# Gate steps ahead of their group, and decay sums ahead of the feed, in a gated linear attention followed by a maxout network

## The chip, the cores and the metric

The kernel runs on one core of one Trainium2 chip. The metric is the device time of one execution in microseconds (us). The kernel before the change took 739.53 us, the median of three runs (738.25 to 742.4). A core has a matrix engine (TensorE, PE in the profile, with its weight loads as PEld), a vector engine (VectorE, DVE), an engine for activation functions (ScalarE, ACT), a general one (GpSimd, POOL) and a queue that only issues transfers here (SyncE, SP). Each engine works through its own instructions in order; they wait for each other by semaphores.

## The reference

For each of 4 batches and 8 heads, a state of 48 x 48 complex numbers is decayed at every one of 768 time steps by a complex gate and takes up the outer product of a key and a value; the query reads its real part. The result, 3072 tokens of 384 numbers, goes through a maxout network.

```python
mag = np.sqrt(a_re * a_re + a_im * a_im)
scale = np.minimum(mag, 0.999) / (mag + 1e-06)
a_re_n, a_im_n = (a_re * scale, a_im * scale)
for t in range(S):
    ar, ai = (a_re_n[:, :, t, :, None], a_im_n[:, :, t, :, None])
    new_re = ar * S_re - ai * S_im
    new_im = ar * S_im + ai * S_re
    kv = np.einsum('bhd,bhe->bhde', k[:, :, t], v[:, :, t])
    S_re, S_im = (new_re + kv, new_im)
    y[:, :, t] = np.einsum('bhd,bhde->bhe', q[:, :, t], S_re)
# ... x: y as (B*S, H*D)
h = np.maximum(np.maximum(x @ w1, x @ w2), x @ w3)
return h @ w_out
```

## The kernel before

The kernel does not step through time. It works on tiles of 128 time steps, with all heads at once, 24 tiles in all; two tiles make a group, three groups a batch. For each tile the gate becomes a logarithm of its size (Ln, the decay) and an angle counted in turns (w). Sums of both over the time steps, made by matmuls with triangular matrices, turn into factors for k and q: the exponentials En and E of the decay sums, and cosine and sine (CS) of the summed turns. With these, a tile's outputs are matrix products within the tile (scores A and B) and with the state g. The network of the tokens before is fed in between as fillers for TensorE.

The gates come in three steps over both tiles of a group. L, w and e are scratch tiles of which there is only one buffer each; Ln has two.

```python
def gate_steps(g, cs):
    # ...
    def s0():
        # ... takes the buffers L, w, e, Ln
        nc.scalar.activation(out=w, in_=ar, func=AF.Square)
        nc.scalar.activation(out=L, in_=ai, func=AF.Square)
        nc.vector.tensor_tensor(out=L, in0=L, in1=w, op=OP.add)
        nc.vector.tensor_scalar(out=L, in0=L, scalar1=SMALL, scalar2=LARGE, op0=OP.max, op1=OP.min)
        act(out=L, in_=L, func=AF.Ln)

    def s1():
        # ...
        act(out=w, in_=L, func=AF.Exp, scale=0.5)
        act(out=e, in_=L, func=AF.Exp, scale=-0.5)
        act(out=e, in_=e, func=AF.Ln, scale=1e-6, bias=1.0)
        nc.scalar.activation(out=L, in_=L, func=AF.Relu, scale=-0.5, bias=lnmax)
        nc.vector.scalar_tensor_tensor(out=part("Ln"), in0=L, scalar=-LNMAX, in1=e, op0=OP.add, op1=OP.add)

    def s2():
        # ...
        nc.scalar.activation(out=e, in_=ar, func=AF.Abs)
        nc.vector.tensor_tensor(out=w, in0=w, in1=e, op=OP.add)
        act(out=L, in_=w, func=AF.Ln)
        act(out=L, in_=L, func=AF.Exp, scale=-1.0)
        (nc.gpsimd if g > 1 else nc.vector).tensor_tensor(out=ai, in0=ai, in1=L, op=OP.mult)
        nc.vector.tensor_tensor(out=w, in0=w, in1=L, op=OP.mult)
        nc.vector.scalar_tensor_tensor(out=w, in0=w, scalar=2.0, in1=ai, op0=OP.subtract, op1=OP.mult)
        nc.scalar.activation(out=ar, in_=ar, func=AF.Sign, bias=tiny)
        nc.scalar.activation(out=ai, in_=ar, func=AF.Copy, scale=-0.25, bias=0.25)
        nc.scalar.activation(out=ar, in_=ar, func=AF.Copy, scale=-1.0 / math.pi)
        # ... less the carry of the group before
    return [s0, s1, s2]
```

The turns and their sums (the tile cs), between two loads of ScalarE's function tables:

```python
def turns(g, cs, meanwhile):
    # ...
    act(out=w[:, lo:hi], in_=w[:, lo:hi], func=AF.Arctan)
    nc.vector.tensor_tensor(out=w[:, lo:hi], in0=w[:, lo:hi], in1=ar[:, lo:hi], op=OP.mult)
    nc.vector.tensor_tensor(out=w[:, lo:hi], in0=w[:, lo:hi], in1=ai[:, lo:hi], op=OP.add)
    meanwhile(2)              # two up steps of the network
    for c in cs:
        ps = banks("cs", DM)
        # ... matmuls of w with triangles of ones; their fractional parts nf

def angles(g, cs, meanwhile=lambda n: None):
    table("trig_and_small")
    turns(g, cs, meanwhile)
    sines(g, cs)
    table("natural_log_exp_and_others")
```

The decay sums of a tile (s0 of products), their exponentials, and the products with k and q on GpSimd; E has two buffers:

```python
    # ... ps = banks("sums"): matmuls of Ln with mid and rest
    act(out=En..., in_=ps[:, :, HC:2 * HC], func=AF.Exp, scale=-1.0)
    for nm, sg in (("k", 1.0), ("q", -1.0)):
        E = nat2.tile([P, DM], FP, tag="E", name="E")
        act(out=E..., in_=ps[:, :, 0:HC], func=AF.Exp, scale=sg)
        eng = nc.gpsimd if g > 1 else nc.vector
        eng.tensor_tensor(out=hd(T[nm, x]), in0=E, in1=hd(T[nm, x]), op=OP.mult)
```

All these matmuls write to psum tiles from one pool of four. `turned(x)` transposes k and q of a tile (turn), copies them from psum on ScalarE, makes the decay factors f (cut, psum tile F) and the new state (psum tile dk, and uk, which is k with its factor En):

```python
def turned(x):
    if x < NX:
        turn(x, "k")
        turn(x, "q")
        cut(x)
    state(x - 1)
    if x < NX:
        products(x)[2]()
        prep(x, 0)

def feed(n):                 # n steps of the network: an up step (tile up, into hT) or an output step (op)
    for _ in range(min(n, len(ffn))):
        ffn.pop(0)()
```

A group, as the source gives its order. `pre` holds the steps for the group after it. TensorE keeps to the order of the source from the second group of this loop on; on the other engines a scheduler picks among what it takes to be ready, by the order of the source.

```python
def group(g):
    x, y = g * C, g * C + 1
    # ... loads; the list of network steps
    pre = pre_steps(g + 1, feed) if g + 1 < NG else [lambda: None] * 8
    gates, sums, (turning,), units = pre[:3], pre[3:5], pre[5:6], pre[6:]
    # ...
    if g > 1:
        feed(1)
    pairs(x)                 # scores A, B and their gathering
    gates[0]()
    gates[1]()
    feed(1)
    turned(y)
    gates[2]()
    feed(1)
    sums[0]()
    sums[1]()
    outputs(x, tokens(x))    # psum tile y, copied to xT
    rest(y)
    turning()                # angles, with two up steps
    pairs(y)
    units[0]()
    units[1]()
    feed(2)
    turned(y + 1)
    feed(1)
    outputs(y, tokens(y))
    rest(y + 1)
    feed(len(ffn))
```

Of the kernel before, what the change touches and what calls it, by code (L numbers as in the profile page):

```python
# [48 lines left out]
def kernel(  # L49
# [22 lines left out]
    C = 2  # L72
# [4 lines left out]
    NG = B * GB  # L77
# [30 lines left out]
    def act(**kw):  # L108
        tab(nc.scalar.activation(**kw))  # L109
# [14 lines left out]
    def banks(nm, n=None):  # L124

        ps = psum.tile([P, 2, 512], FP, tag="ps", name=nm)
        return ps if n is None else ps.rearrange("p a n -> p (a n)")[:, 0:n]
# [139 lines left out]
    def load(g, *parts):  # L267
        for part in parts if g < NG else ():
            for c in range(C):
                part(g, c)  # L270
# [52 lines left out]
    def flat(t):  # L323
        return t.rearrange("p c h d -> p (c h d)")
# [6 lines left out]
    def gate_steps(g, cs):  # L331
        lo, hi = cs[0] * DM, (cs[-1] + 1) * DM

        def part(nm):
            t = T[nm, g]
            return (flat(t) if len(t.shape) == 4 else t)[:, lo:hi]

        def s0():
            if lo == 0:
                for nm in "Lwe":  # L340
                    T[nm, g] = nat1.tile([P, W], FP, tag=nm, name=nm)
                T["Ln", g] = nat2.tile([P, W], FP, tag="Ln", name="Ln")
            L, w, ar, ai = part("L"), part("w"), part("ar"), part("ai")
# [8 lines that stand above are left out]
            L, w, e = part("L"), part("w"), part("e")  # L352
# [8 lines that stand above are left out]
            L, w, e, ar, ai = part("L"), part("w"), part("e"), part("ar"), part("ai")  # L361
# [12 lines that stand above are left out]
            if lo == 0 and g % GB > 0:  # L374
                nc.gpsimd.tensor_tensor(out=ai[0:1, 0:DM], in0=ai[0:1, 0:DM], in1=T["carry", g], op=OP.subtract)

        return [s0, s1, s2]
# [91 lines left out]
    def turn(x, nm):  # L469
        ps = banks("tp", H * P).rearrange("p (s t) -> p s t", t=P)  # L470
        for n in range(H):
            mt(out=ps[0:DD, n], in_=both(T["U" + nm, x], n), identity=ident)
        src = ps[0:DD]
        if nm == "k":
            T["K", x] = un2.tile([P, H, P], FP, tag="K", name="K")
            nc.scalar.copy(out=T["K", x][0:DD], in_=src)  # L476
        else:

            T["Q", x] = un2.tile([P, 4 * H, 48], FP, tag="Q", name="Q")
            nc.scalar.copy(out=T["Q", x][0:DD, :, 0:32], in_=src.rearrange("p s (a t) -> p (s a) t", a=4))  # L480
# [128 lines left out]
    def outputs(x, xs):  # L609

        atm, V, G, QG = T["atm", x], T["v", x], T["G", x], T["QG", x]
        y = banks("y", DM).rearrange("p (k t) -> p k t", k=KD)
        queues = [[] for _ in range(4)]
        for r in range(DM // 32):
            i, w = divmod(r, 3)
            runs = ((0,), (1, 2), (3,))[w]
            for c in range(2):
                todo = [(n, new) for new in (True, False) for n in runs]
                queues[r % 4] += [(r, c, i, n, new, (n, new) == todo[0], (n, new) == todo[-1]) for n, new in todo]
        for todo in zip(*queues):  # L620
            for r, c, i, n, new, start, stop in todo:
                (j, h), lo = divmod(2 * i + n // 2, 4), 32 * n
                mm(out=y[32 * (r % 4):32 * (r % 4) + 32, r // 4, c * L64:(c + 1) * L64],
                                 lhsT=V[:, c, i, lo:lo + 32] if new else G[0:DD, c, i, lo:lo + 32],
                                 rhs=atm[:, 4 * c + h] if new else QG[0:DD, 2 * (4 * c + h) + j], start=start, stop=stop)
        if x == xs[0]:

            T["xT", xs[-1]] = fp2.tile([P, KD, P], FP, tag="ot", name="xT") if len(xs) == 1 else \
                fp2.tile([P, KD, TG], FP, tag="xT", name="xT")
        o = (x - xs[0]) * P  # L630
        nc.scalar.copy(out=T["xT", xs[-1]][:, :, o:o + P], in_=y)
# [32 lines left out]
    def pre_steps(g, *meanwhile):  # L664
        if g >= NG:
            return []
        cs = list(range(C))
        parts = [products(g * C + c) for c in cs]
        return gate_steps(g, cs) + [p[0] for p in parts] + [call(angles, g, cs, *meanwhile)] + [p[1] for p in parts]

    def tokens(x):

        return [x] if x < C else [x // C * C + c for c in range(C)]

    def ffn_steps(xs):

        n = 2 if xs[0] == 0 else 3
        return [call(up_step, xs, range(f, f + n), i) for f in range(0, KF, n) for i in range(3)] \
            + [call(out_step, xs, x) for x in xs]
# [64 lines left out]
    def group(g):  # L744
        x, y = g * C, g * C + 1
        load(g + 1, load_v)
        load(g + 2, load_a, load_kq)
        ffn = held + ffn_steps(tokens(x - 1))
        held[:] = [ffn.pop()]

        def feed(n):
            for _ in range(min(n, len(ffn))):
                ffn.pop(0)()

        pre = pre_steps(g + 1, feed) if g + 1 < NG else [lambda: None] * 8
        gates, sums, (turning,), units = pre[:3], pre[3:5], pre[5:6], pre[6:]

        def pairs(x):
            for f in (scores, gather):
                for nm in "AB":  # L760
                    f(x, nm)
# [12 lines that stand above are left out]
        def rest(x):  # L774
            if x < NX:
                for p in range(1, 4):
                    prep(x, p)

        if g > 1:
            feed(1)  # L780
        pairs(x)
        gates[0]()
        gates[1]()
        feed(1)
        turned(y)
        gates[2]()
        feed(1)
        sums[0]()
        sums[1]()
        outputs(x, tokens(x))  # L790
        rest(y)
        turning()
        pairs(y)
        units[0]()
        units[1]()
        feed(2)
        turned(y + 1)
        feed(1)
# [4 lines that stand above are left out]
    for g in range(1, NG):  # L803
        if g == 2:
            T["chain"] = None
        group(g)
# [32 lines left out]
```

## Time and profile before

| | before |
|---|---|
| median of three runs | 739.53 us |
| span of the profiled execution | 738.4 us |
| network's up matmuls, TensorE busy | 294.0 us |
| network's output matmuls, TensorE busy | 100.5 us |
| TensorE's waits for the turns w ahead of cs | 53.9 us in 12 waits |
| TensorE's waits for Ln ahead of the decay sums | 21.9 us in 4 waits |

The page divides the span in 40 slices; each digit is the busy share of a slice in tenths, and PEclk the clock that TensorE was granted, in tenths of full speed:

```profile
PE   1255588499899899899899899899999899999998
PEld 0144476378778778778778778678778778778785
DVE  5899898776775785775766776776766776756111
ACT  6678665565665565555655555555555555422000
POOL 9200300501302302301303203102204104100000
PEclk9968799899999999999999999999999999999999
```

The first eight slices or so, some 150 us, are the start: weights are loaded and the first group is prepared. Then come the groups, and in the last slices only the network's matmuls are left. In other views, a row that shows a wait has its length and what ended it in brackets.

### The profile page before, as it was taken

Reading aid. Unit: us, or ns where it says so; the run is one execution under the profiler, and the core shown is the slowest. Engines: PE = TensorE matmul, PEld = TensorE weight load, DVE = VectorE, ACT = ScalarE, POOL = GpSimd, SP = SyncE. Lnnn points to the kernel's source line nnn. Section 1 sums busy time; section 2 is a strip of 40 time slices with the busy share of each in tenths; the row PEclk is TensorE's granted clock in tenths of the full one; section 3 lists DMA queues with packets and bytes.
Section 4 is the critical chain, followed back from the end, with each engine's and each line's share of the span. In section 5 each row is a group of like instructions: output and inputs, shape, how many; then the busy total and the mean of one; then the engine's idle time right before and its main releaser. Section 6 shows DMA issues by size and latency. Waiting matters only on the chain.

```text
span 738.4 us, 25162 instructions
## 1 busy us (share of the span) xinstructions
PE 636.7 (86%) x11196; PEld 521.5 (71%) x11196; DVE 506.1 (69%) x695; ACT 391.5 (53%) x617; POOL 134.8 (18%) x121
## 2 busy tenths in 40 slices
PE   1255588499899899899899899899999899999998
PEld 0144476378778778778778778678778778778785
DVE  5899898776775785775766776776766776756111
ACT  6678665565665565555655555555555555422000
POOL 9200300501302302301303203102204104100000
PEclk9968799899999999999999999999999999999999
DMA  8555452131231230230320230221321030000000
GB/s 207 148 122 147 95 132 44 22 71 33 55 60 24 51 60 23 52 60 22 58 59 23 49 64 21 54 57 24 61 55 24 11 67 3 1 25 3 4 21 21
DMA packets 138285, 39.41 MB, mean 53 GB/s; under 512 B 130880, under 2 KB 133952, under 8 KB 138176
## 3 DMA queue, kind: packets, MB, share of 16 engines
q1 hardware_dynamic: 137664, 37.78, 23.3%
q8 instruction: 88, 1.44, 0.8%
q14 instruction: 21, 0.17, 0.1%
q10 hardware_dynamic: 512, 0.01, 0.0%
HBM read 33.03 MB, written 4.72 MB: 51 GB/s over the span
## 4 chain that ended last, share of the span: by engine, by line
PE 42%; issue 28%; ACT 9%; DVE 8%; POOL 6%; SPq 3%; DMA 3%; POOLq 0%; ACTq 0%; DVEq 0%
PE up L114 18%; PE op L114 8%; PE cs L114 4%; PE y L114 3%; PE tp L114 3%; POOL q L454 2%; PE B L114 2%; DMA vb<-in_v_dram 2%; POOL ai L367 2%; SPq L255 1%; PE dk L114 1%; PE A L114 1%; ACT f L109 1%; ACT L130 1%; POOL k L454 1%
## 5 line engine op out<-in xcount | busy, mean ns | idle before, releaser
L114 PE MATMUL up<-xT,w 128*128 128x256 f32 (+1 forms) x1404 | 294.0, 367 | 5.5 <-DVE hT L649 4.8
L114 PEld LDWEIGHTS up<-xT,w 128*128 128x128 f32 x1404 | 247.3, 190 | 39.8 <-DVE hT L649 5.5
L367 POOL TENSOR_TENSOR ai<-ai,L 128x768 f32<-128x768 f32 x10 | 29.8, 2980 | 420.1 <-ACT L L109 369.3
L114 PE MATMUL op<-wo,hT 128*128 128x384 f32 x288 | 100.5, 499 | 1.5 <-DVE wo L321 1.0
L114 PE MATMUL cs<-w,upto 128*64 128x192 f32 x192 | 35.6, 425 | 53.9 <-DVE w L385 53.9
L649 DVE TENSOR_TENSOR hT<-hT,up 128x768 f32<-128x768 f32 (+2 forms) x54 | 46.5, 861 | 47.1 <-PE up L114 47.0
L114 PEld LDWEIGHTS op<-wo,hT 128*128 128x128 f32 x288 | 53.3, 192 | 35.5 <-DVE wo L321 1.1
L507 DVE TENSOR_TENSOR Q<-Q,f 112x512 f32<-112x512 f32 x48 | 33.0, 689 | 49.9 <-ACT f L109 49.8
L114 PEld LDWEIGHTS cs<-w,upto 128*64 128x64 f32 x192 | 21.9, 174 | 62.6 <-issue 35.8
L647 ACT COPY hT<-up 128x768 f32<-128x768 f32 (+2 forms) x27 | 19.6, 727 | 81.3 <-PE up L114 81.1
L507 DVE TENSOR_TENSOR QB<-Q,f 112x512 f32<-112x512 f32 (+1 forms) x48 | 58.2, 1248 | 0.0
L476 ACT COPY K<-tp 112x1024 f32<-112x1024 f32 x24 | 24.3, 1012 | 45.6 <-PE tp L114 44.9
L114 PE MATMUL y<-QG,g 112*32 112x64 f32 x1536 | 46.9, 222 | 1.0 <-DVE g L607 1.0
L114 PE MATMUL y<-atm,vb 128*32 128x64 f32 x1536 | 47.6, 224 | 0.0
L114 PEld LDWEIGHTS y<-atm,vb 128*32 128x32 f32 x1536 | 39.9, 112 | 9.6 <-issue 4.5
L464 DVE TENSOR_TENSOR uk<-uk,En 128x768 f32<-128x768 f32 x24 | 23.0, 959 | 31.9 <-PE tp L114 31.9
L396 ACT ACTIVATE t<-cs 128x384 f32<-128x384 f32 x24 | 11.8, 491 | 56.7 <-PE cs L114 56.7
L114 PEld LDWEIGHTS y<-QG,g 112*32 112x32 f32 x1536 | 40.2, 112 | 1.6 <-DVE g L607 1.6
L109 ACT ACTIVATE f<-F 48x296 f32<-48x296 f32 x96 | 39.6, 413 | 0.8
L507 DVE TENSOR_TENSOR QG<-Q,f 112x1024 f32<-112x1024 f32 x24 | 36.4, 1517 | 0.0
L398 DVE SCALAR_TENSOR_TENSOR nf<-t,cs 128x384 f32<-128x384 f32 x24 | 13.3, 554 | 33.4 <-ACT t L396 33.4
L109 ACT ACTIVATE E<-sums 128x384 f32<-128x384 f32 x48 | 22.1, 490 | 24.3 <-POOL k L454 12.8
(111 smaller groups left out, 1098.5 us busy)
## 6 DMA issues: line engine op xcount, KB each, us to landing
ar<-in_a_re_dram SPq DMA_DIRECT2D x24, 192.0 KB, 2.9
ai<-in_a_im_dram SPq DMA_DIRECT2D x24, 192.0 KB, 4.2
k<-in_k_dram SPq DMA_DIRECT2D x96, 48.0 KB, 2.4
q<-in_q_dram SPq DMA_DIRECT2D x96, 48.0 KB, 2.5
vb<-in_v_dram SPq DMA_DIRECT2D x192, 24.0 KB, 2.1
out_dram<-ot SPq DMA_DIRECT2D x24, 192.0 KB, 2.3
raw<-in_moe_w_dram SPq DMA_DIRECT2D x5, 768.0 KB, 5.4
raw<-in_moe_w_out_dram SPq DMA_DIRECT2D x3, 768.0 KB, 4.9
```

Source lines behind the costliest of these rows:

```text
L109: tab(nc.scalar.activation(**kw))
L114: ins = f(**kw)
L130: tab(nc.scalar.preload_act_table_set(nm))
L367: (nc.gpsimd if g > 1 else nc.vector).tensor_tensor(out=ai, in0=ai, in1=L, op=OP.mult)
L396: nc.scalar.activation(out=t, in_=ps, func=AF.Copy, bias=MAGIC)
L398: nc.vector.scalar_tensor_tensor(out=nf, in0=t, scalar=MAGIC, in1=ps, op0=OP.subtract, op1=OP.subtract)
L454: eng.tensor_tensor(out=hd(T[nm, x]), in0=E, in1=hd(T[nm, x]), op=OP.mult)
L464: nc.vector.tensor_tensor(out=u, in0=u, in1=two(T["En", x]), op=OP.mult)
L476: nc.scalar.copy(out=T["K", x][0:DD], in_=src)
L507: nc.vector.tensor_tensor(out=out, in0=in_, in1=f.to_broadcast([DD, 2 * H, n, 8]), op=OP.mult)
L647: nc.scalar.copy(out=dst, in_=ps)
L649: nc.vector.tensor_tensor(out=dst, in0=dst, in1=ps, op=OP.max)
```

## The change

The first two gate steps are moved out of the group ahead of theirs. Group g now does them for group g + 2, in its second half, behind the products that end the work on the angles; by then the single buffers L, w and e have served group g + 1. The third step, for group g + 1, stands at the beginning of group g, ahead of the network step and the turned tile. In the first group of the loop all three steps of the next group stand at that place, since no group ahead of it has done them. The decay sums of both tiles come directly behind the turned tile, ahead of the network step that stood before them. No operation is added or left out. The aim is that ScalarE, VectorE and GpSimd are through with the gates, and the sums' exponentials begun, before the angles need them.

```diff
         gates, sums, (turning,), units = pre[:3], pre[3:5], pre[5:6], pre[6:]
+        later = gate_steps(g + 2, list(range(C)))[:2] if g + 2 < NG else []
@@
         if g > 1:
             feed(1)
         pairs(x)
-        gates[0]()
-        gates[1]()
+        for f in gates if g == 1 else gates[2:]:
+            f()
         feed(1)
         turned(y)
-        gates[2]()
-        feed(1)
         sums[0]()
         sums[1]()
+        feed(1)
         outputs(x, tokens(x))
         rest(y)
         turning()
         pairs(y)
         units[0]()
         units[1]()
+        for f in later:
+            f()
         feed(2)
         turned(y + 1)
         feed(1)
```

## The prediction

> **What bounds the kernel now.** I first read the page's busy times, then the table of stretches between one cumulative-sum stage (cs) and the next, then the waits of TensorE, and last the order on ScalarE ahead of one such wait. The busy times:
>
> ```profile
> PE 636.7 (86%) x11196; PEld 521.5 (71%) x11196; DVE 506.1 (69%) x695; ACT 391.5 (53%) x617; POOL 134.8 (18%) x121
> ```
>
> TensorE is the longest and the rest is far from full, but 86% mixes a slow start with a steady part. One group of two tiles is the stretch from one start of the cs matmuls to the next (columns: stretch, length, then busy us and instructions of PE, PEld, DVE, ACT, POOL, granted clock, DMA share, GB/s):
>
> ```profile
> 195.68:249.32 53.64, 50.88 (x924) 41.79 (x925) 38.00 (x48) 30.84 (x48) 11.38 (x6) 1.00 0.23 46
> 249.32:304.57 55.25, 52.31 (x924) 42.56 (x925) 39.30 (x51) 30.76 (x48) 11.43 (x6) 0.97 0.23 45
> 304.57:359.19 54.62, 52.37 (x924) 42.78 (x925) 37.28 (x51) 30.73 (x48) 9.51 (x6) 0.97 0.23 45
> 359.19:413.26 54.07, 50.94 (x925) 41.72 (x925) 37.89 (x48) 30.85 (x48) 11.44 (x6) 1.00 0.23 47
> 413.26:469.18 55.92, 52.36 (x924) 42.58 (x925) 40.26 (x51) 30.84 (x48) 8.71 (x6) 0.97 0.23 45
> ```
>
> The group takes 54 to 56 us, of which TensorE is busy for 51 to 52.4. The same matmuls cost 50.9 us where the clock was 1.00 and 52.3 where it was 0.97. The timeline of TensorE, cut to matmul rows that begin with idle time (in brackets, with what ended it), shows the gaps:
>
> ```profile
> 304.57 1.78 PE L114 MATMUL cs<-w,upto 128*64 128x192 f32 x10 [2.48 <-DVE w L385]
> ...
> 349.38 8.04 PE L114 MATMUL up<-xT,w 128*128 128x256 f32 x36 [0.48 <-DVE hT L649]
> 359.19 1.16 PE L114 MATMUL cs<-w,upto 128*64 128x192 f32 x10 [1.77 <-DVE w L385]
> ```
>
> Each group has one wait of 1.8 to 3.1 us for the turns w ahead of cs and about 0.5 us for a maximum on VectorE. The clock belongs to the first: after the 1.77 us gap ten cs matmuls take 1.16 us, after 2.48 us they take 1.78. So in this trace a longer gap costs a second time, as slow matmuls behind it.
>
> Why is w late? ScalarE's timeline ahead of the 1.77 us gap (start, length, line, tiles):
>
> ```profile
> 340.97 1.69 ACT L109 ACTIVATE f<-F 48x296 f32<-48x296 f32 x4
> 342.69 0.84 ACT L109 ACTIVATE L<-w 128x768 f32<-128x768 f32 x1
> 343.56 0.84 ACT L109 ACTIVATE L<-L 128x768 f32<-128x768 f32 x1
> 347.50 0.84 ACT L345 ACTIVATE L<-ai 128x768 f32<-128x768 f32 x1 [3.10 <-POOL ai L367]
> 348.50 0.84 ACT L372 ACTIVATE ai<-ar 128x768 f32<-128x768 f32 x1
> 349.37 0.84 ACT L373 ACTIVATE ar<-ar 128x768 f32<-128x768 f32 x1
> 350.23 0.49 ACT L109 ACTIVATE En<-sums 128x384 f32<-128x384 f32 x1
> 350.62 0.87 ACT L109 ACTIVATE E<-sums 128x384 f32<-128x384 f32 x2
> 351.36 0.51 ACT L109 ACTIVATE En<-sums 128x384 f32<-128x384 f32 x1
> 353.09 0.49 ACT L109 ACTIVATE E<-sums 128x384 f32<-128x384 f32 x1 [1.22 <-POOL k L454]
> 354.36 0.49 ACT L109 ACTIVATE E<-sums 128x384 f32<-128x384 f32 x1 [0.78 <-POOL q L454]
> 354.87 1.28 ACT L130 ACT_TABLE_LOAD   x1
> 356.17 0.84 ACT L109 ACTIVATE w<-w 128x768 f32<-128x768 f32 x1
> ```
>
> This is the path. Behind the turned tile's factors f come the rest of the third gate step (Ln, Exp, 3 us for GpSimd's product, then three passes), then the decay sums' exponentials, paced by GpSimd, then the table load, the arctangent (356.17), and two VectorE passes of about 1 us (to 359.05). The sums' matmuls had ended at 346.96, 3.3 us before their first exponential. Thus w hangs on ScalarE and GpSimd in series, not on the DMA.
>
> **What the Trainium skill says.** "TensorE: Matmul & The Clock Gate", section "Part 1: The HAM clock gate", says that TensorE falls to half clock after an idle activity window of about 3.4 us and needs about as long to recover. The effect agrees, but here gaps of 2.47 to 3.09 us already cost it: granted clock 0.50 in 469 to 472 us behind the 3.09 us gap, 1.00 behind 1.77. "PSUM — Partial Sum Buffer", section "Engine vs sequencer instructions", says that the queues of ScalarE, VectorE and GpSimd are strictly first in, first out. This agrees: ScalarE idles 3.10 us ahead of 347.50, and the exponentials queued behind, whose sums were done at 346.96, run only from 350.23. "ScalarE: Activation LUTs", section "What ACT_TABLE_LOAD costs", gives 1283 ns for the load: 1.28 us here. No load is added. "Perfetto Trace Analysis", section "Optimization Strategy", says to find the gaps of the limiting engine and make what they wait for start sooner. This is what the change does.
>
> **The change part by part.** It adds and removes no arithmetic: the instruction listings of the two builds have the same 1814 rows on TensorE, 518 on ScalarE and 98 on GpSimd; only the order differs.
>
> (a) *Gate steps earlier.* The source placed all three in the first half, but the scheduler had drawn much of the first two into the second half already (the trace has the squares at 309.91 and 347.50, Ln and the Exps at 323.40 to 326.63). So the new part is smaller than the diff looks: in the listing of after the five ScalarE passes of step two stand ahead of the K and Q copies of the next group's first tile, and the third step's Ln and Exp directly behind its f, no longer behind the second tile's. Out of the path go Ln to ar's copy: from 342.69 to 350.23, 7.5 us.
>
> (b) *Sums one feed earlier.* The sums' matmuls (1.46 us) stand directly behind dk and ahead of an up step of 4.1 us. They are then ready 4.1 us earlier.
>
> Now the new group by hand, with this trace's durations at full clock, t = 0 at cs. TensorE without waits: cs to 2.8, A and B to 5.1, two up steps to 13.0, K transposes to 13.9, Q to 14.8, F to 15.2, dk to 16.2, op to 20.3, y to 22.2, op to 26.3, A and B to 28.2, one up to 32.2, transposes to 34.1, F, dk to 35.5, sums to 37.0, up to 41.1, y to 43.2, two up to 51.2, and cs again.
> ScalarE in the second tile's part: K and Q copies 33.1 to 34.9, f to 36.6, En and two E to 37.8; the other two E follow GpSimd (in this trace 1.9 us to the third and 1.3 more to the fourth) and end at 41.2; table load to 42.5, arctangent to 43.3. VectorE: product, a maximum that now stands between, sum: to 46.2. TensorE asks for w at 51.2, 5 us later. The cs wait should go, and with it the slow clock. The 0.5 us maximum wait should go too: in the listing that maximum no longer stands behind the third step's product, which waits for GpSimd.
>
> What the move may cost: table load ends at 8.1 us, five passes to 12.3, Ln on VectorE to 13.2, |ar| to 14.0, K to 14.9, Q to 15.8, f to 17.5. Four psum tiles rotate, so op at 16.2 needs K's copy (14.9), y at 20.3 needs Q's, the second op at 22.2 needs f: all hold, by 1.3 us or more. Tighter is dk, which wants uk at 15.2 and gets it at about 15.1 after Ln and a maximum on VectorE, and the up step at 28.2, which wants xT at 26.9. I allow 0.5 us a group for such misses.
>
> The sum, from the waits of TensorE in the eight steady groups (195.68 to 632.54, 436.86 us): eight cs waits are 18.3 us, the other waits 4.5, and five groups of slow clock 5 x (52.29 - 50.84) = 7.3; that is 30.1, and leaves 8 x 50.84. With 8 x 0.5 = 4 given back the gain is 26. Ahead of them: the cs of the third group stands 10.97 us idle at 146.76. There the first group in a loop gets only part of the change; by hand the third step's Exp comes 1.4 us earlier, w about 2.2 us earlier. The next stretch loses its 1.76 and 0.47 us waits but may pay 1 us for its f, now behind the five passes: 1.2 net. The start and the stretch behind 632.54 have no moved work: 0. Total 26 + 2.2 + 1.2 = 29.5 us, 739.5 - 29.5 = **710 us**.
>
> **The rivals.** *The five passes ahead of K and Q stall TensorE.* For it: queues go in order, and K, Q and f come about 2.5 us later against the transposes. Against it: only psum and dk notice within the half, and ScalarE is busy 31 of 54 us. If op or dk wait 2 us a group, 16 instead of 4 us are lost: 722 us. *The wait moves to another link.* If GpSimd's product slips, xT behind it holds up the up step in two of three orders. At 3 us a group nothing would be left but the cleaner clock: 730 us. *TensorE's clock comes down under unbroken load.* Against it: in the last 106 us of before it was 101 us busy at clock 1.00. With nothing lost anywhere it would be 705 us.
>
> **Range and chances.** The gain's ceiling is well fixed (the waits are listed), the loss is my estimate between 0 and 2 us a group. This gives 705 to 722 us. For less than 2% (over 724.7) more than half of the gain must be eaten: 0.09; slower by 2% would need 1.8 us of new waits a group beyond all that is gained: 0.01.
>
> **What would show it.** Right: groups of 51 to 51.5 us at clock 1.00, no cs wait on L385 in them, arctangent some 8 us ahead of cs, the sums' exponentials directly behind f. Wrong: new TensorE waits on K copies, on uk (L464) or on xT (L631); cs waits still there, then behind GpSimd; the cs idle near 147 us not shortened.

## Result and profile after

The changed kernel takes 714.88 us (median, 714.05 to 717.09), the kernel before in the same comparison 740.96: a ratio of 0.9656, 95% interval 0.9616 to 0.9697. The profiled spans are 712.3 and 738.4 us. The page's busy times of after:

```profile
PE 631.8 (89%) x11196; PEld 517.9 (73%) x11196; DVE 510.0 (72%) x695; ACT 388.6 (55%) x617; POOL 119.1 (17%) x121
```

TensorE has the same instructions and 5 us less to do, from the clock; the other 21 us were idle time. The table of stretches from cs to cs, for the first one in the loop and two that follow (columns as in the prediction):

```profile
145.02:196.87 51.85, 47.08 (x913) 38.62 (x913) 38.26 (x51) 28.97 (x46) 8.75 (x6) 0.94 0.24 46
196.87:247.85 50.98, 50.77 (x925) 41.69 (x924) 38.26 (x47) 30.53 (x48) 8.76 (x6) 1.00 0.25 48
...
298.81:349.55 50.74, 50.62 (x925) 41.59 (x924) 38.34 (x50) 30.50 (x48) 8.69 (x6) 1.00 0.25 49
```

In the two lower rows TensorE is idle 0.1 to 0.2 us of 51, at clock 1.00: no wait worth removing is left there. The top row is another matter: 4.8 us idle and a clock of 0.94. The span splits at the same cs in both kernels:

| us | before | after | difference | predicted |
|---|---|---|---|---|
| start to the cs that waits longest in the loop | 146.76 | 145.02 | -1.7 | -2.2 |
| next stretch | 48.92 | 51.85 | +2.9 | -1.2 |
| eight steady groups | 436.86 | 408.66 | -28.2 | -26.1 |
| behind the last cs | 105.86 | 106.77 | +0.9 | 0 |
| sum | 738.4 | 712.3 | -26.1 | -29.5 |

Why the steady wait is gone is seen on ScalarE ahead of the cs at 349.55 (timeline of after):

```profile
333.65 1.68 ACT L109 ACTIVATE f<-F 48x296 f32<-48x296 f32 x4
335.36 0.49 ACT L109 ACTIVATE En<-sums 128x384 f32<-128x384 f32 x1
335.74 0.87 ACT L109 ACTIVATE E<-sums 128x384 f32<-128x384 f32 x2
...
337.34 0.49 ACT L109 ACTIVATE E<-sums 128x384 f32<-128x384 f32 x1 [0.34 <-POOL k L454]
338.74 0.49 ACT L109 ACTIVATE E<-sums 128x384 f32<-128x384 f32 x1 [0.91 <-POOL q L454]
339.25 1.28 ACT L130 ACT_TABLE_LOAD   x1
340.54 0.84 ACT L109 ACTIVATE w<-w 128x768 f32<-128x768 f32 x1
```

Between f and the first En nothing stands any more; before, the third step's Ln to its three passes stood there for 7.5 us. The arctangent starts 9.0 us ahead of cs (349.55 - 340.54) instead of 3.0 us. Of these 9.0 us VectorE uses up a good part, though, as its timeline shows:

```profile
339.05 2.02 DVE L507 TENSOR_TENSOR KB<-K,f 112x1024 f32<-112x1024 f32 x1
...
341.45 2.17 DVE L507 TENSOR_TENSOR QB<-Q,f 112x512 f32<-112x512 f32 x2
...
344.01 0.95 DVE L384 TENSOR_TENSOR w<-w,ar 128x768 f32<-128x768 f32 x1
...
345.74 0.95 DVE L385 TENSOR_TENSOR w<-w,ai 128x768 f32<-128x768 f32 x1
```

The arctangent is done at 341.38, but VectorE comes to L384 only at 344.01, because KB and QB stand ahead of it. They run while GpSimd multiplies k and q (338.67 to 341.93) and are slow: KB takes 2.02 us here, 1.22 in before at 349.25, where GpSimd was idle. QG does the reverse: 2.02 us in before beside GpSimd, 1.21 here behind it. The Trainium skill says this under "SBUF — State Buffer", section "Who interferes with whom": a VectorE instruction with two inputs in SBUF contends with a GpSimd instruction that reads it. So w is ready at 346.69, 2.9 us before it is asked for.

### The profile page after: what moved, and what is told of

It reads as the page before. It is cut to its first block, busy times and chain, and to the rows that moved or that the text cites. A ratio compares the mean times of both kernels' runs of the same rounds, so it can differ in the third digit from the quotient of the medians.

```text
span 712.3 us, 25175 instructions
## 1 busy us (share of the span) xinstructions
PE 631.8 (89%) x11196; PEld 517.9 (73%) x11196; DVE 510.0 (72%) x695; ACT 388.6 (55%) x617; POOL 119.1 (17%) x121
## 3 DMA queue, kind: packets, MB, share of 16 engines
q8 instruction: 88, 1.44, 0.9%
## 4 chain that ended last, share of the span: by engine, by line
PE 56%; ACT 16%; DVE 12%; issue 10%; SPq 3%; POOL 1%; ACTq 1%; DMA 1%; POOLq 0%
PE up L114 27%; PE op L114 12%; PE cs L114 5%; DVE Q L507 3%; PE y L114 3%; DVE KB L507 3%; PE B L114 3%; ACT f L109 3%; PE tp L114 3%; ACT K L476 2%; ACT CS L109 2%; PE dk L114 2%; PE A L114 2%; ACT Q L480 2%; ACT e L109 2%
## 5 line engine op out<-in xcount | busy, mean ns | idle before, releaser
L367 POOL TENSOR_TENSOR ai<-ai,L 128x768 f32<-128x768 f32 x10 | 24.3, 2426 | 322.0 <-ACT L L109 265.0
L507 DVE TENSOR_TENSOR Q<-Q,f 112x512 f32<-112x512 f32 x48 | 40.8, 851 | 42.8 <-ACT f L109 42.7
L114 PE MATMUL cs<-w,upto 128*64 128x192 f32 x192 | 31.0, 381 | 29.4 <-DVE w L385 29.4
L114 PEld LDWEIGHTS cs<-w,upto 128*64 128x64 f32 x192 | 19.0, 156 | 36.6 <-issue 19.5
L507 DVE TENSOR_TENSOR KB<-K,f 112x1024 f32<-112x1024 f32 x24 | 37.3, 1553 | 0.0
L114 PE MATMUL sums<-Ln,mid 64*64 64x192 f32 x192 | 15.0, 363 | 25.1 <-DVE Ln L357 23.8
L454 POOL TENSOR_TENSOR k<-E,k 128x384 f32<-128x384 f32 x20 | 23.7, 1186 | 76.6 <-ACT E L109 76.6
L114 PE MATMUL B<-QB,KB 112*32 112x80 f32 x1536 | 32.6, 237 | 2.5 <-DVE QB L507 2.2
```

The costliest lines, as they stand in the source:

```text
L114: ins = f(**kw)
L507: nc.vector.tensor_tensor(out=out, in0=in_, in1=f.to_broadcast([DD, 2 * H, n, 8]), op=OP.mult)
```

## Experiments

All ratios are to the kernel before, run beside each on the same chip. "Steady" is the sum of the eight groups of the table, 436.86 in before and 408.66 in after.

**Which part brings the gain?** The change has three: steps one and two go two groups ahead, step three goes to the front, the sums go ahead of a feed. The first experiment is before with step three moved alone:

```diff
         gates[1]()
+        gates[2]()
         feed(1)
         turned(y)
-        gates[2]()
         feed(1)
```

> The kernel before with one line moved: the third gate step ahead of the network step and the turned tile, as the two others are; sums behind the feed as before, nothing two groups ahead. Theory A (what counts is that the third step's Ln, Exp, GpSimd product and three passes leave ScalarE's path behind f; steps one and two were drawn early by the scheduler anyway): cs waits of the steady groups gone or under 0.3 us, groups near 51.2 us at clock 1.00, 713 to 718 us. Rival B (it takes steps one and two in the group ahead): waits stay at 1.8 us or more, 735 us or more. Rival C (both the gates and the sums are needed): waits halved, about 725 us.

Measured: 717.88 us, 0.9696 (0.9655 to 0.9737). No cs wait in the steady groups, clock 1.00, steady 413.52. The third step's place alone brings 23.3 of the 28.2 us. The second is before with the sums moved alone:

```diff
         turned(y)
-        gates[2]()
-        feed(1)
         sums[0]()
         sums[1]()
+        gates[2]()
+        feed(1)
```

> The kernel before with the decay sums directly behind the turned tile and the third gate step behind them, then the feed. By hand from the trace of before: the exponentials run from 342.7 instead of 350.2, in the time in which ScalarE idled; Ln, Exp, table load and GpSimd's product follow; w at about 357 where cs is asked for at 357.4. Theory A: the waits shrink to 0 to 0.8 us a group, 714 to 722 us. Rival C (both parts needed): waits of 1 us and more, clock still falling in some groups, 725 us or more.

Measured: 742.14 us, 1.0031 (1.0 to 1.0062), steady 439.12, and a cs wait of 2.5 to 2.9 us in every group. The expectation failed. ScalarE, GpSimd, VectorE and TensorE ahead of one cs (a fence for each timeline of this run):

```profile
346.42 0.84 ACT L109 ACTIVATE L<-w 128x768 f32<-128x768 f32 x1
347.29 0.84 ACT L109 ACTIVATE L<-L 128x768 f32<-128x768 f32 x1
348.15 1.28 ACT L130 ACT_TABLE_LOAD   x1
353.95 0.84 ACT L345 ACTIVATE L<-ai 128x768 f32<-128x768 f32 x1 [4.51 <-issue]
...
355.71 0.83 ACT L109 ACTIVATE w<-w 128x768 f32<-128x768 f32 x1
```

```profile
349.19 2.25 POOL L367 TENSOR_TENSOR ai<-ai,L 128x768 f32<-128x768 f32 x1
```

```profile
348.76 3.77 DVE L507 TENSOR_TENSOR QB<-Q,f 112x512 f32<-112x512 f32 x2
...
352.92 0.95 DVE L368 TENSOR_TENSOR w<-w,L 128x768 f32<-128x768 f32 x1
```

```profile
359.40 1.16 PE L114 MATMUL cs<-w,upto 128*64 128x192 f32 x10 [2.48 <-DVE w L385]
```

The exponentials of the sums do come early, but the third step's Exp now ends behind them (348.13). GpSimd's product, behind the k and q products, ends at 351.44, VectorE's L368 stands behind a QB that GpSimd slows, and ScalarE's L345, whose output is the same scratch tile L that L368 reads, idles until 353.95 with the arctangent behind it. The wait has moved to another link, and w is as late as ever. The third is after without its two other parts, so that only steps one and two are ahead:

```diff
-        for f in gates if g == 1 else gates[2:]:
+        for f in gates[:2] if g == 1 else []:
             f()
         feed(1)
         turned(y)
+        gates[2]()
+        feed(1)
         sums[0]()
         sums[1]()
-        feed(1)
```

> The changed kernel with only its first part: steps one and two in the second half of the group two ahead, but the third step behind the turned tile and the sums behind the feed, as before. Theory A: nothing of the path is shortened, cs waits of 1.8 to 3.1 us and the slow clock stay, 735 to 742 us. Rival B (steps one and two early are what helps): 715 to 720 us.

Measured: 742.99 us, 1.0074 (1.0049 to 1.0099), steady 437.13, cs waits of 1.75 to 3.09 us as in before. Steps one and two were not what w waited for. Two more runs leave out one part each. Before with step three and the sums early and nothing two groups ahead:

```diff
         gates[1]()
-        feed(1)
-        turned(y)
         gates[2]()
         feed(1)
+        turned(y)
         sums[0]()
         sums[1]()
+        feed(1)
```

> The kernel before with the third gate step ahead of the network step and the turned tile and the sums directly behind it, in every group; no step two groups ahead. Theory A (third step and sums out of the path are all of the gain; the part with the steps two groups ahead is idle): groups of 50.8 to 51.3 us, whole time 712 to 716 us, no worse than the changed kernel. Rival B (the steps two groups ahead matter beside them): 718 us or more.

Measured: 717.04 us, 0.973 (0.9673 to 0.9787), steady 410.84; the time lies between what the two theories asked for. And after with the sums behind the feed again:

```diff
         turned(y)
+        feed(1)
         sums[0]()
         sums[1]()
-        feed(1)
```

> The changed kernel with the sums behind the network step as before. Third step alone, without the sums, took the cs waits away already (717.9 us). Theory A: no cs waits in the steady groups, w ready within 1.5 us of being asked for, 714 to 719 us. Rival C (with the steps two groups ahead the sums' move is needed): cs waits of 1 us and more, 722 us or more.

Measured: 718.18 us, 0.9736 (0.9671 to 0.98), steady 414.14. The cs waits stay away, but dk waits 0.4 to 1.5 us in six groups, 6.1 in all (after has 1.5 in all). What the two other parts bring on top of step three is not shown. The steady sums fall by 2.7 us (413.52 to 410.84) and 5.5 us (414.14 to 408.66) where the sums come early. But the first difference lies in stalls of TensorE for which the trace names no releaser (4.5 us in the run with step three alone, 1.0 with the sums early), and 4.6 of the second in the dk waits, which hang on something else (below). The steps two groups ahead take away five small waits for VectorE at F, 2.2 us in all, and bring the dk waits. By their times' intervals these last versions can't be told apart.

**Why is the next stretch longer?** TensorE's rows with waits in it, in the timeline of after:

```profile
178.01 1.14 PE L114 MATMUL dk<-vb,uk 64*64 64x48 f32 x64 [0.87 <-ACT hT L647]
179.65 0.56 PE L114 MATMUL sums<-Ln,mid 64*64 64x192 f32 x8 [0.50 <-ACT K L476]
...
181.30 0.56 PE L114 MATMUL sums<-Ln,mid 64*64 64x192 f32 x8 [0.76 <-ACT Q L480]
...
182.87 1.35 PE L114 MATMUL up<-xT,w 128*128 128x256 f32 x5 [0.69 <-ACT f L109]
```

Four waits one behind the other, all for ScalarE, and this is what ScalarE does meanwhile:

```profile
172.01 0.85 ACT L109 ACTIVATE L<-w 128x768 f32<-128x768 f32 x1 [4.21 <-DVE w L363]
172.88 0.84 ACT L109 ACTIVATE L<-L 128x768 f32<-128x768 f32 x1
176.43 0.84 ACT L345 ACTIVATE L<-ai 128x768 f32<-128x768 f32 x1 [2.70 <-POOL ai L367]
177.18 0.78 ACT L647 COPY hT<-up 128x768 f32<-128x768 f32 x1
...
178.60 1.00 ACT L476 COPY K<-tp 112x1024 f32<-112x1024 f32 x1
```

The third step's Ln waits 4.21 us for VectorE, its product another 2.70 on GpSimd, and the network's copy hT and the K and Q copies stand in the queue behind. In this group, with the sums right behind the turned tile, the third step at the front is too early. The test is after with the old place in the second group of the loop alone:

```diff
-        for f in gates if g == 1 else gates[2:]:
+        for f in gates if g == 1 else gates[2:] if g != 2 else []:
             f()
         feed(1)
         turned(y)
+        if g == 2:
+            gates[2]()
         sums[0]()
         sums[1]()
```

> The changed kernel, but in the second group of the loop alone the third gate step stands behind the turned tile again (sums behind it). In the changed kernel that stretch (145.02 to 196.87) took 51.85 us against 48.92 before, with 4.8 us of small waits of TensorE, which I put down to ScalarE: Ln of w waits for VectorE, GpSimd's product follows, and the hT, K and Q copies stand behind both. If so the stretch falls to 48 to 49.5 us and the whole to 711 to 713 us. Rival: the five passes of steps one and two ahead of f are the cause; then the stretch stays at 51 us or more and the time at 714 to 715.

Measured: 713.54 us, 0.9637 (0.9595 to 0.968); the stretch takes 49.45 us instead of 51.85. The whole time can't be told apart from that of after, and is a little more than was expected: the steady groups of this trace take 410.46 us, with 3.3 us of dk waits. ScalarE in it, timeline of this run:

```profile
176.68 0.80 ACT L647 COPY hT<-up 128x768 f32<-128x768 f32 x1 [7.07 <-PE up L114]
177.55 1.01 ACT L476 COPY K<-tp 112x1024 f32<-112x1024 f32 x1
178.46 1.02 ACT L480 COPY Q<-tp 112x1024 f32<-112x1024 f32 x1
179.37 1.69 ACT L109 ACTIVATE f<-F 48x296 f32<-48x296 f32 x4
```

Now ScalarE waits for TensorE, not the other way round, and K follows the up step's copy at once; the waits of dk, sums and up are gone. The price is a cs wait of 1.10 us at the stretch's end, contained in the 49.45. The five passes of the steps for the group after next still stand ahead of this group's first f, so they are not the cause.

The third step's place costs that much only together with the sums'. With step three in front and the sums behind the network step the stretch took 49.41 us (step three alone moved) and 49.95 (sums behind the feed again), and TensorE did not wait for Q and f there. With both early it took 50.54 without the steps two groups ahead, and 51.85 in after.

**Is the slow clock caused by the gap?** If so, filling the gap with useless matmuls must bring time back. Six of them were put ahead of each steady group's cs in before, into the psum tile that cs then overwrites.

```diff
             ps = banks("cs", DM)
+            if c == 0 and g > 2:
+                for _ in range(6):
+                    mm(out=ps, lhsT=ident, rhs=ws[0][:, 0, 0:DM], start=True, stop=True)
```

> The kernel before with six extra matmuls of constants (2.1 us, their result is overwritten) in TensorE's gap ahead of cs in the steady groups; the gap's end is set by w as before. Clock theory (gaps of 2.5 us and more cost a slow clock behind them, 1.45 us a group in five groups): clock 1.00 in all steady groups, their busy time without the extra matmuls 50.8 us, and the time falls by 5 to 7 us to 732 to 735. Rival (the slow clock has another cause, or the gap alone counts): 739 to 742 us.

Measured: 746.65 us, 1.0121 (1.0074 to 1.0168). The clock was 1.00 in every group, but the fill was too long: one such matmul shows as two of 0.33 us, so that six took 4.0 us where the gaps are 1.8 to 3.1. With three (only the 6 changed to 3):

> As the run with six extra matmuls, but three: each had turned out to be two instructions of 0.33 us, so six took 4.0 us and overfilled the gap. Three take 2.0 us, inside it. There the clock was 1.00 in all groups and a group took 55.0 us, of which 4.0 were the extra matmuls. Clock theory: clock 1.00 again, the gap of 1.8 to 2.5 us is filled and not lengthened, groups of 53.3 to 54.0 us instead of 54.6 on average, 6 us saved, 731 to 736 us. Rival (no gain from the clock, since w is late by the same time after the group's start anyway): 738 us or more.

Measured: 733.76 us, 0.993 (0.991 to 0.9951). TensorE's timeline at one cs of this run:

```profile
301.65 2.10 PE L114 MATMUL cs<-w,ident 128*128 128x384 f32 x6
304.19 1.19 PE L114 MATMUL cs<-w,upto 128*64 128x192 f32 x10 [0.44 <-DVE w L385]
```

The fill takes 2.10 us of the gap and leaves 0.44, w is no earlier against the matmuls ahead of it, and the ten cs matmuls take 1.19 us instead of up to 2.15. TensorE does more work in less time: the groups come to 53.59 us on average instead of 54.61, all at clock 1.00. This is the clock's share of the gap, shown by itself: 8 us in the eight groups of the trace, 5.2 between the medians (738.96 and 733.76). The same was then tried on the long gap of the loop's first cs, on top of the version with the old place in group two, first with 18 matmuls:

```diff
             ps = banks("cs", DM)
+            if c == 0 and g == 2:
+                for _ in range(18):
+                    mm(out=ps, lhsT=ident, rhs=ws[0][:, 0, 0:DM], start=True, stop=True)
```

> The changed kernel with the third step of the loop's second group back behind the turned tile (713.5 us alone), and eighteen extra matmuls of constants (6.2 us, their result is overwritten) in the 6.6 us gap ahead of the cs of the loop's first group. Clock theory: the cs, A and B matmuls behind it run at full clock, 2 to 2.7 us are saved, 710 to 712 us. Rival (what comes behind waits for other engines anyway): 713 to 714 us.

Measured: 715.0 us, 0.9693 (0.9648 to 0.9737): 11.8 us of fill for a gap of 6.6 put the cs off to 152.19, while the stretch behind it took 46.71 us instead of 49.45. With nine (the 18 changed to 9):

> As the run with eighteen extra matmuls in the loop's first group, but nine: those took 11.8 us and put off cs to 152.2; nine take 5.9 us in a gap of 6.6. Clock theory: cs, A and B behind it at full clock, cs still at 146 to 147, 2 to 2.7 us saved against 713.5: 710.5 to 712 us. Rival: 713 us or more.

Measured: 710.74 us, 0.9624 (0.9583 to 0.9665). After itself was run once more beside it:

> The changed kernel once more, on the same chip as the two beside it: 714 to 716 us, with at most two small waits at dk in the steady groups.

Measured: 714.82 us (713.02 to 716.12), 0.9686 (0.9647 to 0.9724). Its trace also tells how far two traces of one kernel lie apart: the cs at 146.62 instead of 145.02, the next stretch 51.57 instead of 51.85, the steady groups 407.70 instead of 408.66, and one dk wait of 0.38. The runs with nine matmuls lay between 708.78 and 712.25, all below those of after on the same chip. Stretches of after, behind its 6.58 us gap:

```profile
145.00:149.00 4.00, 3.98 (x21) 3.15 (x22) 0.90 (x2) 0.49 (x1) 0.00 (x0) 0.50 0.95 187
149.00:151.00 2.00, 2.00 (x38) 1.28 (x39) 0.01 (x1) 0.53 (x2) 0.00 (x0) 0.50 0.02 4
151.00:155.00 4.00, 4.00 (x129) 3.88 (x122) 3.95 (x7) 3.95 (x8) 0.00 (x0) 1.00 0.03 6
```

and the whole stretch in the old-place version without the fill and with it (one fence for each):

```profile
146.82:196.27 49.45, 46.40 (x912) 38.56 (x913) 36.37 (x50) 29.91 (x47) 9.38 (x6) 0.94 0.24 46
```

```profile
147.86:194.58 46.72, 43.70 (x913) 36.88 (x913) 36.45 (x50) 29.91 (x47) 9.38 (x6) 1.00 0.25 49
```

In after, half clock lasts 6 us behind the gap. The fill takes it away: the same matmuls keep TensorE busy for 43.70 instead of 46.40 us, and this difference of 2.70 is the stretch's whole gain of 2.73.

**What do the remaining dk waits hang on?** They come in some groups only. ScalarE and then TensorE in such a group, timelines of after:

```profile
557.57 2.17 ACTq L404 DMA_DIRECT2D carry<-nf  x2
559.78 0.61 ACT L109 ACTIVATE CS<-af,biases 128x384 f32<-128x384 f32 x1 [1.69 <-DVE atm L554]
```

```profile
569.66 1.14 PE L114 MATMUL dk<-vb,uk 64*64 64x48 f32 x64 [1.11 <-DVE hT L649]
```

ScalarE issues two small transfers of the carry; here this held it 2.17 us, in the group at 353.57 only 1.17, and there dk waits for nothing. The releaser named for the first CS is a guess of the profile: the activation begins as the issue ends. The sizes fit. In the traces of after and of five other versions with the steps two groups ahead, each issue that took 1.44 us or more, 18 in all, was followed by a dk wait of its length less 1.05 to 1.07 us (here 2.17 and 1.11). One group had a dk wait of 0.37 or 0.38 us with an issue of only 1.15 in three of these traces, so that one has another cause. In before and in the run with step three alone moved, issues of up to 2.16 us brought no dk wait in the steady groups: there the five passes of steps one and two come behind K and Q, and ScalarE's idle time ahead of K (5.44 us in before at 319.87) takes up the issue. The test is the version with nine matmuls and the carry on the transfer queue:

```diff
-                    nc.scalar.dma_start(out=T["carry", g + 1][:, j * HC:(j + 1) * HC], in_=nf[last - 1:last, HC:])
+                    nc.sync.dma_start(out=T["carry", g + 1][:, j * HC:(j + 1) * HC], in_=nf[last - 1:last, HC:])
```

> The fastest version so far (third step of the loop's second group behind the turned tile, nine extra matmuls ahead of the first cs of the loop; 710.7 us) with the two small transfers of the carry issued by SyncE instead of ScalarE. In the traces ScalarE's issue of them took 1.2 us in some groups and 2.2 to 2.6 in others, and where it was long TensorE waited at dk (0.4 to 1.5 us). Theory: ScalarE's stall of about 0.7 to 2 us behind the second t goes, no dk waits are left in the steady groups, 708 to 710.5 us. Rival: the dk waits have another cause, or the carry comes later and holds up GpSimd's subtraction: 710.5 us or more.

Measured: 709.3 us (708.13 to 711.09), 0.9647 (0.9625 to 0.9669; before took 735.94 on that chip). All eight groups take 50.73 to 50.82 us, 406.06 in all (409.43 without the move), and no dk waits. But the second cs of all came at 88.0 instead of 84.2 us, and the loop's first at 150.28 instead of 147.86, so that 2.4 of the 3.4 us are lost again; why the start is longer was not pursued. By time the two versions can't be told apart. Both beat before; that the one with the carry on SyncE beats after is not shown, since their ratios' intervals overlap.

## Why the prediction was right, and where it was not

The total, 710 against 714.88 us, was within the range, and most steps hold: the gain in the groups comes from the path that was named. But the gain in the trace is 26.1 and not 29.5 us, and two larger errors, 2.1 us too little in the steady groups and 4.1 too much in the next stretch, partly cancel; so far the closeness is luck.

- *Steady groups, 26 predicted, 28.2 measured.* The path was the right one: cs waits gone, the waits of 0.5 us for a maximum gone, clock 1.00, exponentials directly behind f. The mis-sized term is the allowance of 0.5 us a group for misses: 408.66 - 8 x 50.84 leaves 0.24 a group.
- *"7.3 us of slow clock"* was argued from a few gaps. The fills show that the clock does come from the gap and can be had back without moving any w (8 us in the trace of the run with three matmuls).
- *"The next stretch ... 1.2 net": this step failed;* the stretch became 2.9 us longer. The prediction asked for the 1 us that f would lose behind the five passes, and overlooked that step three, put in front, holds ScalarE's queue for 4.21 us of waiting for VectorE and 2.70 for GpSimd, with K, Q and f behind, which the sums and the step after them now ask for at once. Undone in that group alone, 2.4 us came back. The 0.5 us that remain against before are TensorE's own: it is busy for 46.40 us there and was for 45.60 in before, because half clock lasts some 6 us behind the gap now and lasted some 4.6 before (0.50 in 146.76 to 151, 0.95 in 151 to 155). That may be chance: half clock lasted 5.2 us at this place in the second run of after.
- *First cs in the loop, 2.2 predicted, 1.7 measured,* and only 0.1 in the second trace of after (146.62), where the start had been 0.8 us later (its second cs at 83.04 instead of 82.23). ScalarE did better than predicted: its arctangent starts at 138.66 instead of 143.00. VectorE gave most of it back, timeline of after:

```profile
136.98 2.02 DVE L507 TENSOR_TENSOR KB<-K,f 112x1024 f32<-112x1024 f32 x1
138.92 2.62 DVE L507 TENSOR_TENSOR QB<-Q,f 112x512 f32<-112x512 f32 x2
141.46 1.21 DVE L507 TENSOR_TENSOR QG<-Q,f 112x1024 f32<-112x1024 f32 x1
142.59 0.94 DVE L384 TENSOR_TENSOR w<-w,ar 128x768 f32<-128x768 f32 x1
...
143.93 0.95 DVE L385 TENSOR_TENSOR w<-w,ai 128x768 f32<-128x768 f32 x1
```

  The arctangent ends at 139.50, and w waits 3.1 us in VectorE's queue behind KB, QB and QG, which before had run while ScalarE was still behind. w is complete 1.7 us earlier (144.88 instead of 146.61). The 6.58 us wait seems 4.4 us shorter than before's 10.97, but 2.0 us of it have only moved ahead, to the sums, which wait 2.31 instead of 0.3 us for Ln at 126.16. An order with L384 and L385 ahead of KB and QB was not tried.
- *"TensorE asks for w at 51.2, 5 us later": 2.9.* The same queue, and VectorE's instructions slowed beside GpSimd, whose work now falls together with theirs. It cost nothing here, as slack was left.
- *The tight points.* dk was named as tight and is the only steady wait left (1.5 us in two groups), though what used up its slack was the issue of the carry, which the hand schedule had left out, and not Ln and the maximum. xT caused no wait.
- *The rivals.* Five passes ahead of K and Q stall nothing by themselves, and in the bad stretch they were not the cause; but they leave dk so little slack that a long issue of the carry becomes a wait (5.7 us in the eight groups of the run with the sums behind the feed). TensorE's clock stays at 1.00 through the 408.66 us of the eight groups. The wait that moves to another link did not come with the whole change, but it is exactly what came when the sums were moved alone. The prediction had not split the change, and counted on the sums, ready 4.1 us earlier; no run shows a clear gain from them.
- *Behind the last cs, 0 predicted, 0.9 lost.* A clock of 0.96 in the last 17 us (1.00 in before) and a wait of 0.3 us ahead of B are seen there. This part took 106.5 us in the second run of after, and 106.2 and 107.8 in the two runs without a gain (steps one and two ahead, sums early), so that 0.9 is not clear of the spread; the cause is open.

## What to carry to other kernels

When a serial chain over several engines is late, moving a link that isn't the last to arrive brings nothing, or only hands the wait on; find the link that ends last and move that, one part at a time if the parts can be had singly. What is moved to the front of an in-order queue brings its own waits along, so look at the groups at the ends of a loop, where its inputs are later than in the steady ones. Where a gap of 2 to 3 us on TensorE can't be closed, a few matmuls on data that lie ready, fewer than fill it, can save the slow clock behind it.

## What was not expected of the hardware

- The gap's length alone doesn't decide on the slow clock, and the first ten matmuls don't tell whether it came, as it can begin about a microsecond behind the gap's end. Behind the 2.48 us gap of before at 249.32 they took 1.16 us (full speed), and the clock fell after them (windows of before):

```profile
249.32:250.32 1.00, 1.00 (x11) 0.92 (x11) 0.72 (x1) 0.08 (x1) 0.00 (x0) 1.00 0.96 186
250.32:253.32 3.00, 3.00 (x15) 2.21 (x13) 0.55 (x1) 0.41 (x1) 0.00 (x0) 0.50 0.99 196
```

  All five gaps of 2.47 to 3.09 us of before were followed by 3.0 to 3.4 us of half clock, and none of the gaps of 1.75 to 1.81 us in the traces was. But in the run with the sums moved alone a gap of 2.87 us was followed by 10 us at clock 1.00 (579.85 to 590), and so were gaps of 2.38, 2.48 and 2.47 in the run with steps one and two ahead. Nor does the gap set how long half clock lasts: some 4.6 us behind the 10.97 us gap of before and 5.2 behind the same gap in the run with steps one and two ahead, 6 and 5.2 behind the 6.58 us gap in the two runs of after. What else decides is open.
- VectorE beside GpSimd: the same KB or QG product takes 1.21 to 1.22 us alone and 2.02 us beside it, the QB pair mostly 1.82 and up to 6.45 (before, at 459.05, where GpSimd's four products ran at 0.98 to 0.99 us each meanwhile).
- The issue of two small transfers held ScalarE for 1.2 us in one group and 2.2 in another of the same run. SyncE issued nothing during the 2.2 us; why it differs is open.
